# A new order for the opening of an attention and Fourier mixing kernel, with copies, queries, combinations and conversions of its first group at other places

## The chip, the cores and the metric

The kernel runs on one core of one Trainium2 chip. The metric is device time in microseconds (us), the median of the runs shown; lower is better. One further execution was taken under the hardware profiler, and all lines below that quote a trace come from it.

## The reference

The first stage is an attention whose softmaxes are taken over the query's features and over the key's positions, the second a Fourier mixing block with a two layer network. There are 8 batches of 576 positions and 8 heads of 64, so rows of 512:

```python
q_s = softmax(q, axis=-1)
k_s = softmax(k, axis=2)
kv = np.einsum('bhsd,bhse->bhde', k_s, v)
x = np.einsum('bhsd,bhde->bhse', q_s, kv)      # then laid out as (8, 576, 512)
...
mixed = np.real(np.fft.fft(np.fft.fft(x, axis=1), axis=2))
u = x + mixed
un = (u - mean(u)) / np.sqrt(var(u) + 1e-06)
out = u + np.maximum(un @ w_ch1, 0.0) @ w_ch2  # 512 to 2048 to 512
```

(Both softmaxes subtract the maximum and add 1e-9 to the sum; `softmax` stands for those three lines.) All is float32; the host hands the two weight matrices over as 64 bit words, and the kernel converts them to float32.

## The kernel before

**Tiling.** Each batch has 576 positions. Four tiles of 128 of them, called (c, u) with c and u in 0 and 1, are a batch's own; the other 64 of each batch are put together with those of the next batch into a "shared" tile of 128. The own tokens of a batch make a group of 512 columns for the network. There are nine groups: group 0 is batch 0, the eight others follow, the last two of them being the shared tokens and batch 7.

**Stages.** The opening (`opening`, L576, with `first_keys`, L516) does the attention of batch 0, its Fourier mixing (`folded`, `block`, `mix_own`) and its normalisation (`norm`, L1070). In the opening the four own query tiles are called A (0, 0), B (1, 1), C (0, 1) and D (1, 0), and the shared one t. Keys and values of batch 0 and 1 are k00 to k03 and k10 to k13: for each the maximum (max), the exponential (exp), four transposes (turn), their copy out of PSUM (four), and the product with v (kv, L560). "k0 last" and "k0 fifth" handle the last positions of all four, "k0 inverse" and "k0 scale" (L564) finish the key times value matrix. A query has max, less (subtract), exp, turn, copy, ones (L880, its sums), kv (L888), inverse and out (L903). Then tokens, columns, by and again (L949 to L969) fold rows and columns, b0 to b4 (L1001, L1004) are the first Fourier product, m0 and m1 (L1029, with sums in L1046) the second, and s, root, scales, normal (L1100 on VectorE, L1103 on ScalarE), turn (L1109) and laid (L1117) are the normalisation and its transposes for the network.

The first group of the network (`plain`, L1154) uses plain products: 16 blocks of L1163, each with a relu on ScalarE (L1168), then 64 products L1175 into four PSUM banks, in the order of the list DOWN. During this group the weights are converted for the first time (`weights`, L329; conversion i is c_i: L376 on ScalarE, L370 and L373 on VectorE, L377 on ScalarE, L378 on GpSimd; 0 to 15 are the first matrix and 16 to 31 the second), and the sums of weight blocks that the later groups need are formed and stored to DRAM (`combine`, L396: four L428 on VectorE and the stores L431 to L437; layer 0 writes w1s, layer 1 writes w2s, eight p of each). The attention and the mixing of batch 1 run beside it. The later groups use a fast matrix product with seven products for eight (`strassen`, L1192; L1237 in the first layer, L1448, L1333 and L1363 in the second), whose weights come from DRAM through `load` (L449, issued at L455).

**What sets the order.** No scheduler decides. Every step has a time in a list; the kernel sorts the steps by it and issues them (end of the main function), and each engine takes its own instructions strictly in that order. In the opening the times stand in the string OPENING. WARM adds, at the given times, so many matmuls that are not used (L242). After the opening the times are offsets from `first` (start of the first group) and t = first + second (start of its second half). DMAs are issued in the same way from the queue of SyncE (SP), a few in the opening from that of ScalarE.

**Buffers that matter.** The transposes have two PSUM banks (tag tr), the products acc three. Query tiles have three buffers (tag q) and their transposes two (qT). The combinations for p = 2 and 6 of layer 1 write to s1 and u2, which the fast product uses too; the others write to parts of the first matrix that are no longer needed, or to the buffer unT that is not yet used. The slots into which `load` writes are parts of that same first matrix.

## Time and profile before

| | before |
|---|---|
| median of 3 runs | 1087.71 us (1086.84 to 1087.93) |
| the profiled execution | 1088.17 us |
| its span, first to last instruction | 1086.4 us |
| mean granted TensorE clock | 0.997 |
| matmul passes | 6390 |
| DMA traffic | 236.29 MB, mean 218 GB/s |

The same by stage (busy us, from the windows of the trace):

| stage | us | TensorE | VectorE | ScalarE | GpSimd | GB/s |
|---|---|---|---|---|---|---|
| opening | 0 to 54.6 | 46.72 | 36.37 | 32.13 | 14.66 | 246 |
| first group, L1163 | 54.6 to 112.2 | 57.41 | 44.67 | 35.96 | 26.86 | 247 |
| first group, L1175 | 112.2 to 188.1 | 72.16 | 64.34 | 33.37 | 16.34 | 249 |
| second group | 188.1 to 307.3 | 119.20 | 69.20 | 43.91 | 51.45 | 224 |
| the rest | 307.3 to 1086.4 | 768.36 | 453.30 | 260.04 | 351.71 | 209 |

How to read it: a busy time is a sum over the instructions of an engine; a matmul in float32 is recorded as two passes, and neighbouring passes overlap a little, so TensorE's busy time says that it was working, not that it worked at its peak. In the lines of the trace that follow, "x8" counts passes. The name after an arrow in brackets is what ended the idle time before an instruction. The clock is a share of full speed.

### The profile page before, as it was taken

The page shows a single profiled execution, that of the slowest core. Times are in us where ns is not written, and L with a number is a line of the kernel's source. Part 1 is how long each engine was busy: PE and PEld are TensorE (multiplying, and loading weights), DVE is VectorE, ACT ScalarE, POOL GpSimd, SP SyncE. Part 2 cuts the span into 40 slices and gives each one's busy share as a digit, 9 for nine tenths or more (in the row PEclk, how much of TensorE's full clock was granted, in tenths as well). Part 3 has the DMA queues.
Part 4 walks back from the last instruction along what each step waited for, and adds up shares of the span by engine and source line. Part 5 has one row for each costly group of instructions (what it writes and reads, how often), then busy time and mean ns, then how long its engine had stood idle before and what let it go on. Part 6 is the DMA issues. An engine that isn't in the chain of part 4 may idle for free.

```text
span 1086.4 us, 16999 instructions
## 1 busy us (share of the span) xinstructions
PE 1063.9 (98%) x6390; PEld 922.5 (85%) x6390; DVE 667.9 (61%) x1285; ACT 405.4 (37%) x962; POOL 461.0 (42%) x377
## 2 busy tenths in 40 slices
PE   8899999999999999999999999999999999999997
PEld 7744454988888899889998998889988998899896
DVE  5877896565465775667654765677447742562251
ACT  5674732552235215531444234521552132131200
POOL 3153220146323644354624642374336353553343
PEclk9999999999999999999999999999999999999999
DMA  9477577466996567645765566557644674666473
GB/s 337 158 233 271 217 261 241 148 219 202 294 315 234 186 227 261 207 159 210 262 220 189 185 235 219 186 208 253 219 165 155 214 248 159 219 236 214 165 244 125
DMA packets 114785, 236.29 MB, mean 218 GB/s; under 512 B 24320, under 2 KB 76160, under 8 KB 104080
## 3 DMA queue, kind: packets, MB, share of 16 engines
q1 hardware_dynamic: 112896, 234.15, 63.2%
q10 hardware_dynamic: 1808, 1.06, 0.3%
q8 instruction: 51, 0.84, 0.3%
q14 instruction: 30, 0.25, 0.1%
HBM read 200.05 MB, written 39.32 MB: 220 GB/s over the span
## 4 chain that ended last, share of the span: by engine, by line
PE 83%; DVE 5%; ACT 2%; issue 1%; POOL 1%; DVEq 0%; ACTq 0%; POOLq 0%
PE bb L1237 15%; PE bb L1363 10%; PE bc L1237 10%; PE ba L1237 10%; PE bc L1363 6%; PE ba L1363 6%; PE bb L1333 4%; PE acc L717 2%; PE acc L888 2%; PE bb L1448 2%; PE bc L1175 2%; PE acc L1001 2%; PE acc L1004 2%; PE acc L1029 1%; PE bc L1448 1%; PE ba L1448 1%
## 5 line engine op out<-in xcount | busy, mean ns | idle before, releaser
L1237 PE MATMUL bb<-unT,big 128*128 128x256 f32 x768 | 183.9, 379 | 0.0
L384 POOL TENSOR_TENSOR big<-big 128x512 f32<-128x512 f32 x32 | 40.9, 1279 | 284.7 <-ACT big L1249 284.7
L1237 PEld LDWEIGHTS bb<-unT,big 128*128 128x128 f32 x768 | 142.8, 190 | 18.6 <-DVE u L1207 0.4
L1249 ACT ACTIVATE big<-big 128x512 f32<-128x512 f32 x96 | 60.4, 629 | 199.7 <-DVE big L1248 199.5
L1207 DVE TENSOR_TENSOR u<-bb,s 128x512 f32<-128x512 f32 x66 | 45.6, 691 | 131.1 <-PE bb L1237 113.8
L1237 PE MATMUL bc<-unT,big 128*128 128x256 f32 x512 | 123.9, 379 | 0.0
L1237 PE MATMUL ba<-unT,big 128*128 128x256 f32 x512 | 123.8, 379 | 0.0
L1363 PE MATMUL bb<-big 128*128 128x128 f32 x848 | 105.2, 275 | 2.3 <-DVE u L1370 2.3
L1237 PEld LDWEIGHTS ba<-unT,big 128*128 128x128 f32 x512 | 94.7, 190 | 12.4 <-issue 0.5
L1237 PEld LDWEIGHTS bc<-unT,big 128*128 128x128 f32 x512 | 94.4, 190 | 12.3 <-DVE big L1248 0.8
L1363 PEld LDWEIGHTS bb<-big 128*128 128x128 f32 x848 | 99.6, 192 | 2.9 <-DVE u L1370 2.9
L1309 DVE TENSOR_TENSOR big<-big 128x512 f32<-128x512 f32 x92 | 83.0, 945 | 5.9 <-POOL big L385 3.4
L1313 POOL TENSOR_TENSOR x<-x,big 128x512 f32<-128x512 f32 x52 | 68.0, 1318 | 28.0 <-ACT big L1340 14.8
L1363 PE MATMUL ba<-big 128*128 128x128 f32 x640 | 79.6, 275 | 0.0
L1363 PEld LDWEIGHTS ba<-big 128*128 128x128 f32 x640 | 76.3, 192 | 1.2
L770 ACT ACTIVATE q<-q,qm 128x64 f32<-128x64 f32 x240 | 65.2, 338 | 27.1 <-DVE qm L764 20.6
L1309 POOL TENSOR_TENSOR big<-big 128x512 f32<-128x512 f32 x26 | 41.2, 1596 | 74.1 <-DVE big L1309 53.8
L1370 DVE TENSOR_TENSOR u<-bb,s 128x256 f32<-128x256 f32 x40 | 16.9, 423 | 70.5 <-PE bb L1363 61.8
L1333 PE MATMUL bb<-big 128*128 128x256 f32 x256 | 58.7, 380 | 0.0
L1248 DVE TENSOR_TENSOR big<-bc,u 128x512 f32<-128x512 f32 x64 | 44.0, 687 | 23.7 <-PE bc L1237 22.6
L1333 PEld LDWEIGHTS bb<-big 128*128 128x128 f32 x256 | 48.2, 190 | 8.0 <-DVE big L1248 1.1
L1363 PE MATMUL bc<-big 128*128 128x128 f32 x416 | 51.5, 275 | 0.0
(260 smaller groups left out, 2030.9 us busy)
## 6 DMA issues: line engine op xcount, KB each, us to landing
big<-w2d SPq DMA_DIRECT2D x67, 1024.0 KB, 4.8
big<-w1s SPq DMA_DIRECT2D x64, 896.0 KB, 4.9
big<-w2s SPq DMA_DIRECT2D x16, 1024.0 KB, 6.3
big<-in_w_dram SPq DMA_DIRECT2D x21, 512.0 KB, 6.2
w2d<-big SPq DMA_DIRECT2D x42, 256.0 KB, 5.6
q<-in_q_dram SPq DMA_DIRECT2D x27, 256.0 KB, 6.5
k<-in_kT_dram SPq DMA_DIRECT2D x24, 288.0 KB, 5.7
v<-in_v_dram SPq DMA_DIRECT2D x24, 256.0 KB, 3.6
```

Source lines behind the costliest of these rows:

```text
L384: e1.tensor_tensor(out=to(4), in0=at(2), in1=at(3), op=ALU.add)
L717: nc.tensor.matmul(pk, lhsT=ks[:, c, :], rhs=v[:, c, :], start=(c == 0), stop=(c == NC - 1))
L770: nc.scalar.activation(q[:, h, :], q[:, h, :], ACT.Exp, bias=m[:, h:h + 1])
L1207: plus = lambda t: V.tensor_tensor(out=temp(t), in0=box["bb"][:], in1=box["s1"][:], op=ALU.add)
L1237: nc.tensor.matmul(bank()[:, i, :], lhsT=w[:, WA_AT[m], k * P:(k + 1) * P], rhs=self.unT[g][:, B_AT[m], k, :], start=first and i == 0 and ...
L1248: steps = [(0, lambda: V.tensor_tensor(out=hp(i), in0=bank()[:], in1=u()[:], op=ALU.add)), (0.8, lambda: nc.scalar.activation(hp(i), hp(i) ...
L1249: (0.8, lambda: nc.scalar.activation(hp(i), hp(i), ACT.Relu))]
L1309: e.tensor_tensor(out=to(o), in0=to(x), in1=to(y), op=op)
L1313: G.tensor_tensor(out=x, in0=x, in1=tile(m), op=ALU.add)
L1333: nc.tensor.matmul(box[name][:, i, :], lhsT=h[p][:, A_AT[m], i * P:(i + 1) * P], rhs=self.stream[n][:, p, :], start=p == 0 and (m != 1 or ...
L1363: nc.tensor.matmul(box[place[n]][:, i, :], lhsT=own(m)(A_AT[n])[:, f, :], rhs=w[:, r // 2, r % 2 * P:r % 2 * P + P], start=first and f == ...
L1448: nc.tensor.matmul(bank()[:, i, :], lhsT=h[p][:, A_AT[m], i * P:(i + 1) * P], rhs=w[:, p, :], start=first and i == 0 and p == 0, stop=p == ...
```

## The change

The string OPENING and the list WARM are new. In the opening the shared query tile t is handled after the four own ones, and by a subtraction on VectorE and one exponential over 512 columns in place of eight of 64 with a bias each. The load of its first rows (`shared_firsts`) moves from ScalarE's queue to SP's, ahead of the two tables. Two of the four laid copies (those with c equal to u) are done by VectorE and not ScalarE. `first` is 46.9 in place of 48.2, so that all later times move with it. In the first group: conversion 1 is 2.2 later (relative to `first`), the conversions from 23 on are at other times, the combinations p = 6 and 7 of layer 0 come 24.5 later, those of layer 1 in another order and six of them close together near its end, three `load`s at other times, and the queries of batch 1 some 1 to 2.5 earlier; the fourth of these takes a q buffer in place of a piece of unT and is loaded 5.5 earlier.

```diff
--- before.py
+++ after.py
@@ -82,31 +82,30 @@
 PAIRS = [(j + NP // 2, j) for j in range(NP // 2)]
 
 DOWN = [(i, f) for n in range(4) for i in (2, 3, 0) for f in range(4 * n, 4 * n + 4)] + [(1, f) for f in range(NF)]
-WARM = (3, 3), (8.1, 1), (10.85, 1), (26.6, 2), (29, 3), (41.3, 3), (42.8, 2)
+WARM = (3, 3), (24.7, 6), (41.9, 2), (43.45, 1), (44.5, 1), (45.5,2)
 OPENING = """
-4.50 k00 max, 5.30 k00 exp, 5.50 k01 max, 6.25 k00 turn, 6.30 k01 exp, 6.50 k02 max, 7.15 k00 four,
-7.25 k01 turn, 7.60 k03 max, 7.65 k02 exp, 8.41 k01 four, 8.60 k02 turn, 8.91 k03 exp, 9.50 A max,
-9.67 k02 four, 9.86 k0 last, 10.10 B max, 10.25 A less, 10.36 k03 turn, 10.70 k0 fifth, 11.01 k03 four,
-11.29 B less, 11.30 k0 inverse, 11.50 t max, 11.51 A exp, 11.60 k00 kv, 12.25 A turn, 12.25 t exp0,
-12.70 k01 kv, 12.73 t exp1, 13.21 t exp2, 13.40 D max, 13.69 t exp3, 14.00 C max, 14.15 D less, 14.17 B exp,
-14.60 t inverse, 14.67 A copy, 14.82 B turn, 15.19 C less, 15.30 D exp, 15.32 A ones, 15.80 B copy,
-16.12 k02 kv, 16.23 t normal, 16.34 C exp, 16.77 D turn, 16.85 A inverse, 17.22 t turn, 17.72 k03 kv,
-17.87 t copy, 18.37 B ones, 18.52 k0 scale0, 18.97 k0 scale1, 19.17 C turn, 19.32 B inverse, 19.62 A kv,
-19.72 t fold, 20.32 k10 max, 20.42 t join, 20.59 B kv, 20.72 D copy, 20.99 A out, 21.22 k10 exp, 21.56 D ones,
-21.98 C copy, 22.03 B out, 22.36 D kv, 22.65 D inverse, 23.05 k11 max, 23.33 C ones, 23.72 D out,
-23.85 k11 exp, 24.13 C kv, 24.34 C inverse, 24.74 tokens1, 25.10 k11 turn, 25.36 C out, 25.55 k10 turn,
-25.70 k11 four, 25.98 columns1, 26.00 t kv, 26.20 k10 four, 26.34 tokens0, 26.96 tokens2, 27.05 t parts,
-27.58 columns0, 28.06 by1, 28.15 c0 hi, 28.42 by0, 28.78 t folds, 28.80 c0 lo, 29.53 again0, 29.83 again1,
-30.33 tokens3, 30.43 b1 times, 30.95 columns2, 31.31 columns3, 31.41 b4 times, 31.63 b1 copies, 31.79 by3,
-32.15 by2, 32.39 b0 times, 32.61 b4 copies, 32.63 again2, 32.93 again3, 33.43 k13 max, 33.53 b3 times,
-33.59 b0 copies, 34.10 c0 shift, 34.23 k13 exp, 34.51 b2 times, 34.80 c0 sign, 34.99 b3 copies, 35.40 k12 max,
-35.49 k13 turn, 35.52 c0 add, 35.71 b2 copies, 36.26 k12 exp, 36.41 m0 times, 37.02 k13 four, 37.31 k12 turn,
-37.52 m0 copy, 37.76 m1 times, 37.91 k12 four, 38.02 m0 sums, 38.66 k1 last, 38.86 m1 copy, 38.92 m0 add0,
-39.26 k1 fifth, 39.60 m0 add1, 39.60 m1 sums, 39.76 roots, 39.91 k10 kv, 40.40 s00, 40.66 k11 kv,
-40.90 m1 add1, 41.15 s01, 41.41 k12 kv, 42.05 root0, 42.16 k13 kv, 42.20 m1 add0, 42.88 scales0, 43.08 s10,
-43.23 normal01, 43.83 s11, 43.98 turn01, 44.58 normal00, 44.73 root1, 44.93 laid01, 45.08 scales1,
-45.23 turn00, 45.43 normal10, 45.43 normal11, 45.98 laid00, 46.08 turn10, 46.68 turn11, 46.83 laid10,
-47.43 laid11, 49.00 k1 inverse, 49.30 k1 scale0, 49.60 k1 scale1"""
+4.30 k00 max, 5.10 k00 exp, 5.50 k01 max, 6.05 k00 turn, 6.30 k01 exp, 6.65 k02 max, 7.06 k00 four,
+7.25 k01 turn, 7.56 k02 exp, 7.75 k03 max, 8.32 k01 four, 8.51 k02 turn, 8.82 k03 exp, 8.90 A max, 9.50 B max,
+9.58 k02 four, 9.65 A less, 9.77 k0 last, 10.10 k0 inverse, 10.27 k03 turn, 10.42 k0 fifth, 10.69 B less,
+10.80 A exp, 11.20 k00 kv, 11.30 k03 four, 11.84 B exp, 11.85 A turn, 12.20 C max, 12.30 k01 kv, 12.45 A copy,
+12.80 D max, 12.95 B turn, 12.95 C less, 13.40 A ones, 13.55 B copy, 13.99 D less, 14.10 C exp, 14.20 k02 kv,
+14.35 A inverse, 14.85 C turn, 15.00 t max, 15.14 D exp, 15.30 k03 kv, 15.75 t less, 15.95 D turn,
+16.35 k0 scale0, 16.40 B ones, 16.47 t exp, 16.80 k0 scale1, 17.14 t inverse, 17.25 B kv, 17.99 B inverse,
+18.22 A kv, 18.35 C copy, 18.39 t normal, 19.01 B out, 19.19 t turn, 19.32 D copy, 19.63 k10 max, 19.69 C ones,
+19.84 t copy, 20.30 A out, 20.43 k10 exp, 20.49 C kv, 20.92 C inverse, 21.39 t fold, 21.46 D ones,
+22.09 t join, 22.26 D kv, 22.51 D inverse, 22.91 C out, 23.31 t kv, 23.53 D out, 24.15 tokens0, 24.21 k10 turn,
+24.36 t parts, 24.77 tokens1, 25.39 columns0, 25.46 k10 four, 25.75 columns1, 26.23 by1, 26.59 by0,
+26.80 c0 hi, 26.95 t folds, 27.45 c0 lo, 27.70 again0, 28.00 again1, 28.50 tokens3, 28.60 b0 times,
+29.12 tokens2, 29.58 b1 times, 29.74 columns3, 29.80 b0 copies, 30.10 columns2, 30.56 b4 times, 30.58 by2,
+30.78 b1 copies, 30.94 by3, 31.42 again2, 31.72 again3, 31.76 b4 copies, 32.22 k12 max, 32.32 b2 times,
+32.89 c0 shift, 33.02 k12 exp, 33.30 b3 times, 33.59 c0 sign, 33.78 b2 copies, 34.19 k13 max, 34.28 k12 turn,
+34.31 c0 add, 34.50 b3 copies, 34.86 k11 max, 35.05 k13 exp, 35.20 m0 times, 35.81 k12 four, 36.10 k13 turn,
+36.31 m0 copy, 36.55 m1 times, 36.66 k11 exp, 36.81 m0 sums, 37.42 k13 four, 37.61 k1 last, 37.71 m0 add0,
+37.92 m1 copy, 38.07 k11 turn, 38.27 k1 fifth, 38.39 m0 add1, 38.42 m1 sums, 38.77 k11 four, 38.92 k10 kv,
+39.22 s00, 39.27 roots, 39.67 k11 kv, 39.69 m1 add1, 39.97 s01, 40.42 k12 kv, 40.87 root0, 40.99 m1 add0,
+41.17 k13 kv, 41.67 scales0, 41.87 s11, 42.02 normal01, 42.62 s10, 42.77 turn01, 43.37 normal00, 43.52 root1,
+43.87 scales1, 43.89 normal11, 43.95 laid01, 44.02 turn00, 44.22 normal10, 44.77 laid00, 44.87 turn10,
+45.47 turn11, 45.62 laid10, 46.22 laid11, 51.00 k1 inverse, 51.30 k1 scale0, 51.60 k1 scale1"""
 ATT_EPS = 1e-9
 LN_EPS = 1e-6
 
@@ -272,7 +271,7 @@
                 nc.scalar.dma_start(tail[i * Q:(i + 1) * Q], flat[a:a + Q])
 
         def shared_firsts():
-            nc.scalar.dma_start(tail[0:P:Q], self.q[b:b + 2].rearrange("b s n -> (b s) n")[::S // 2])
+            load(tail[0:P:Q], self.q[b:b + 2].rearrange("b s n -> (b s) n")[::S // 2])
 
         def table():
             t = self.small.tile([P, 1], F32, tag="root", name="root", bufs=1)
@@ -298,9 +297,9 @@
             load(t[:, 4, :], self.v[1, S - P:, cols])
 
         order = [lambda: nc.gpsimd.memset(v[0:64, 4, :], 0.0), shared, table, *(lambda r=r: keys(r) for r in range(NR)), lambda: queries(0),
-                 lambda: values(0), lambda: queries(1), lambda: values(2), self.tables,
+                 lambda: values(0), lambda: queries(1), lambda: values(2), shared_firsts, self.tables,
                  *(lambda r=r: second(r) for r in range(NR)), *(lambda i=i: fetch(i) for i in range(11))]
-        return [(8.3, shared_firsts)] + [(i / 100, step) for i, step in enumerate(order)]
+        return [(i / 100, step) for i, step in enumerate(order)]
 
     def shared(self, a, b):
 
@@ -591,7 +590,7 @@
             for name, (_, step) in zip(names, script):
                 steps[name] = step
 
-        named("t max,t exp0,t exp1,t exp2,t exp3", self.q_exp(shared)[:-1])
+        named("t max,t less,t exp", self.q_exp_spread(shared, V))
         named("t inverse,t normal", self.q_inverse(shared, V, V))
         named("t turn,t copy", self.t_turn(shared))
         named("t fold,t join", self.t_fold(shared))
@@ -733,10 +732,7 @@
             if b == 0:
                 self.live[it] = [self.at_start[2][c ^ u][:, u, :]]
                 return
-            if b == 1 and (c, u) == (1, 1):
-                q = self.spare(D)
-            else:
-                q = self.work.tile([P, D], F32, tag="q", name="q", bufs=3)[:]
+            q = self.work.tile([P, D], F32, tag="q", name="q", bufs=3)[:]
             self.nc.sync.dma_start(q, self.q[b, tokens(c, u), :])
             self.live[it] = [q]
 
@@ -799,7 +795,7 @@
 
         return [(0, inverse), (0, times)]
 
-    def q_exp_spread(self, it):
+    def q_exp_spread(self, it, e=None):
 
         nc, live = self.nc, self.live
         heads = lambda: live[it][0].rearrange("p (h d) -> p h d", h=H)
@@ -811,7 +807,7 @@
 
         def less():
             m = live[it].pop()[:].unsqueeze(2).to_broadcast([P, H, DH])
-            nc.gpsimd.tensor_tensor(out=heads(), in0=heads(), in1=m, op=ALU.add)
+            (e or nc.gpsimd).tensor_tensor(out=heads(), in0=heads(), in1=m, op=ALU.add)
 
         def exp():
             q = live[it][0]
@@ -1114,7 +1110,8 @@
                 self.unT[g] = self.work.tile([P, 7, 2, HD], F32, tag="unT", name="unT", bufs=1)
             c, u = i % 2, i // 2
             cols = slice(c * P, (c + 1) * P)
-            nc.scalar.copy(self.unT[g][:, u:u + 3:2, :, cols], box.pop(i)[:].rearrange("p (a k) t -> p a k t", a=2))
+            copy = V.tensor_copy if g == 0 and c == u else nc.scalar.copy
+            copy(self.unT[g][:, u:u + 3:2, :, cols], box.pop(i)[:].rearrange("p (a k) t -> p a k t", a=2))
 
         def combine():
             if g > 0:
@@ -1549,7 +1546,7 @@
         return lazy(lambda: blk.combine(layer, p), 0, 0.4, 0.8, 1.2, 2.2)
 
     groups = [*range(B - 1), B, B - 1]
-    first, second, both = 48.2, 56, 77
+    first, second, both = 46.9, 56, 77
     steps = blk.opening(fetch, converted)
     up, down = blk.plain(0, lambda: blk.unT[0])
     for f in range(NF):
@@ -1557,21 +1554,21 @@
     t = first + second
     for i, some in enumerate(down):
         steps += at(t + 1.2 * i, some)
-    words = [first - 1.9, *(first + 0.9 + 1.7 * i for i in range(NF - 2))]
-    words += [first + dt for dt in (27, 31, 35, 39, 44, 49)] + [t + dt for dt in (-2, 3, 8, 12, 15, 17.2, 29, 32, 35, 38)]
+    words = [first + 0.3, *(first + 0.9 + 1.7 * i for i in range(NF - 2))]
+    words += [first + dt for dt in (27, 31, 35, 39, 44, 49)] + [t + dt for dt in (-2, 2, 5.5, 9, 12, 26, 30, 33, 36, 39)]
     for i, dt in enumerate(words, 1):
         steps += at(dt, converted(i))
-    for p, dt in enumerate((15, 20, 25, 36, 41, 46.5, 59, 62.5)):
+    for p, dt in enumerate((15, 20, 25, 36, 41, 46.5, 83.5, 87)):
         steps += at(first + dt, combined(0, p))
     steps += [(t + 0.5 + 0.1 * i, lambda i=i: fetch(i)) for i in LATE_WORDS]
     steps.append((t + 6, lambda: setattr(blk, "spare_words", blk.raws[LATE_WORDS[0]].bitcast(F32))))
-    steps += [(t + 14 + 4 * i, lambda i=i: blk.load(i)) for i in range(3)] + [(t + 71, lambda: blk.load(3))]
-    for p, dt in zip((3, 0, 1, 7, 2, 4, 5, 6), (30.5, 33.5, 37, 45, 50, 56, 61, 65)):
+    steps += [(t + dt, lambda i=i: blk.load(i)) for i, dt in ((1, 14), (0, 36), (2, 40))] + [(t + 71, lambda: blk.load(3))]
+    for p, dt in zip((3, 7, 0, 1, 2, 4, 5, 6), (34, 42.5, 57.3, 59.3, 61.3, 63.5, 65.5, 68)):
         steps += at(t + dt, combined(1, p))
     own = [("q", 1, c, u) for c in range(2) for u in range(2)]
     for i, it in enumerate(own):
-        at_q = t - 14 + 6 * i
-        steps += at(t - 34 + i if i < 3 else t + 0.6, blk.q_load(it)) + at(at_q, blk.q_exp(it))
+        at_q = t - 15 + 5.5 * i
+        steps += at(t - 34 + i if i < 3 else t - 4.9, blk.q_load(it)) + at(at_q, blk.q_exp(it))
         steps += at(at_q + 9.5, blk.q_turn(it)) + at(at_q + 14, blk.q_times_kv(it))
     steps += at(t + 11, blk.t_times_kv(1)) + at(t + 19.5, blk.folded(1))
     for k, dt in zip((2, 3, 0, 1, 4), (25, 26.5, 29.5, 31, 32.5)):
```

## The prediction

> **What bounds the kernel now.** I read the page first (parts 1 and 2), then who TensorE waited for, then the opening and the first group engine by engine in order of time, then the granted clock by microseconds.

> ```profile
> span 1086.4 us, 16999 instructions
> ...
> PE 1063.9 (98%) x6390; PEld 922.5 (85%) x6390; DVE 667.9 (61%) x1285; ACT 405.4 (37%) x962; POOL 461.0 (42%) x377
> ...
> PE   8899999999999999999999999999999999999997
> ```

> TensorE is busy nearly throughout, and no matmul of the reference is added or removed. So the change can win only where TensorE stands idle or runs slowly: in the opening, before the first L1163 matmul at 54.59, and in the waits of the first group. From 188 us on, TensorE waits only 3.3 us in all (2.3 of it L1363 on DVE), and its order there is untouched. The waits from 54 to 190 us are these (total, times, longest):

> ```profile
> PE acc L1001 <- DVE eo L969: 1.7, 1, 1.7
> PE ba L1163 <- ACT unT L1117: 1.5, 1, 1.5
> PE acc L888 <- DVE big L373: 1.1, 1, 1.1
> PE tr L826 <- issue: 0.6, 1, 0.6
> ...
> PE acc L888 <- ACT qT L836: 0.2, 1, 0.2
> ```

> All but the L1163 line lie between 112 and 141 us, where VectorE is 34.69 us busy of 38; the chain that ended last runs on DVE (L428, L370, L764, L787) from 95 to 140.5. There DVE is the bound.

> The first block of eight L1163 passes (a start, a length) takes 5.37 us, and every later one 3.60; the windows show why (PEclk is the number after POOL's):

> ```profile
> 54.59 5.37 PE L1163 MATMUL ba<-unT,big 128*128 128x512 f32 x8 [1.51 <-ACT unT L1117]
> 59.79 3.60 PE L1163 MATMUL bb<-unT,big 128*128 128x512 f32 x8
> ```
> ```profile
> 52.00:54.00 2.00, 0.66 (x4) 0.42 (x4) 1.03 (x2) 2.00 (x5) 0.00 (x0) 1.00 0.00 0
> ...
> 56.00:57.00 1.00, 1.00 (x2) 0.34 (x1) 0.97 (x3) 0.09 (x1) 0.00 (x0) 0.50 0.31 49
> 57.00:58.00 1.00, 1.00 (x2) 0.34 (x1) 0.97 (x3) 0.00 (x0) 0.81 (x1) 0.50 0.63 233
> ```

> TensorE was idle for most of 52 to 54.6, ACT busy all through, and the clock then fell to half for some 3.4 us: 1.75 us lost.

> [...]0.50 from about 55.3 to 58.7, and 128-column passes of 421 ns until about 14 us, 275 after. [...]here 1.28 at 44.09, before the first root. [...]here an L428 takes 0.41 alone and up to 1.57 beside L378. [...]the nearest row, L549 on DVE, took 0.70.

> **The opening, part by part.** The rows that I start from (ACT, then DVE):

> ```profile
> 8.86 1.13 ACTq L275 DMA_DIRECT2D big<-in_q_dram  x1
> 10.03 0.59 ACT L541 COPY ks<-tr 128x512 f32<-128x512 f32 x1 [1.54 <-PE tr L538]
> 14.82 2.02 ACT L770 ACTIVATE big<-big,qm 128x64 f32<-128x64 f32 x8 [0.64 <-DVE qm L764]
> ```
> ```profile
> 22.18 0.86 DVE L564 TENSOR_TENSOR kvr<-acc,kinv 64x256 f32<-64x256 f32 x2 [2.80 <-PE acc L560]
> 41.97 0.76 DVE L1046 TENSOR_TENSOR eo<-acc,sn 128x256 f32<-128x256 f32 x2 [1.68 <-ACT sn L1038]
> ```

> (1) L275 leaves ACT's queue, where the copy "k01 four" stood behind it until 10.03. It can now start when "k02 exp" ends, at 8.5. Then k03 exp ends at 9.9 (11.4 before), k0 last and k03 turn run cold (1.24 + 1.06) from 9.95, and k00 kv starts at 12.3 instead of 13.67: -1.4.
> (2) On TensorE, k00 kv still runs cold (2.1), then A turn 0.45, k01 kv 1.2, B turn 0.45, ones 0.9, k02 kv 1.2, C turn 0.45, k03 kv 1.15: end 20.2 against 21.98. The shared turn (0.44) and the 0.55 wait are no longer in it. The shared exponentials are one 0.63 instruction instead of 2.02, plus one DVE addition of 0.69 ahead of L564, in idle time. L564 ends at 21.1, not 23.04: -1.9.
> (3) DVE from L564 to "again1" took 11.3 (23.07 to 34.4). It gains the shared inverse 1.05 and normal 0.69, which stood before L564, and gives up k11 max 0.67 and one token sum 0.64: some 12.0. End 33.2: -1.2.
> (4) The token sum and k11 max come back before "again3": 37.1 against 37.64. On ACT, k13 exp 0.97 and k12 four 0.5 stand before m0 copy, so m0 sums (L1046) start at 41.8: -0.2 only. What is late next is ACT.
> (5) From L1046 to the second L1100 is as before, 8.25 (the table load on ACT ends at 46.1, just in time): 49.9, -0.3.
> (6) The tail took 4.37 before (50.22 to 54.59): ACT alone did four L1117 copies (0.58 each), the last L1103, and c1's L376 and L377 between them. Now copies 00 and 11 are on DVE at 0.70 each and c1 waits behind. From 49.9: copy 00 50.45 to 51.1, turn11 to 51.75, copy 11 to 52.45, beside it two warming matmuls (0.86) to 52.6. L1163 starts at 52.65: -1.9 in all.

> The warming matmuls stay 15 in number (0.43 each when warm). They fill the wait for DVE and now also the gaps between the four turns, so the idle window goes and with it the half clock: -1.75. Conversion c1 is due 3.43 after the start: L376 0.65, two L370 and one L373 2.0, L378 1.29 come to about that; +0.2.

> L275 on SP costs up to its 1.13 there, ahead of the tables, the second batch's keys and the words. I take nothing: the DMA share is above 1.0 until 36 us, so transfers and not issue are late. Without that cover: 1.1 on c0.

> **The first group.** Combinations (0,6) and (0,7) leave the stretch from 116 to 125.5: eight L428, 1.85 + 0.41 + 0.42 + 2.70 = 5.4 us of DVE. Conversion 27 (0.42 + 1.69) moves behind the folds. That is 7.5 us less before the L969 that TensorE waits for; the queries go in 1 to 2.5 earlier. Of the waits 1.70 + 1.13 + 0.55 + 0.17 = 3.55 I keep 0.5, for the fourth query, whose exponentials still queue on ACT with conversions: -3.0. The moved 7.5 us fit into DVE's idle time after 141: 1.14 + 3.59 + 4.61 = 9.3. Without it the subtractions L1123 are late for the second product of the next group.

> DMAs that move: the fourth query takes a q buffer, and its load waits for the first query's turn (108.2); behind it on SP are three late words, which before stood behind a load that went at 112.3. The loads of w1s 4 and 5 go some 18 to 22 us later, behind the stores of combinations 6 and 7. They land about 30 us before they are read: nothing.

> **Sum.** -1.9 - 1.75 + 0.2 - 3.0 = -6.45. The profiled execution took 1088.17 (span 1086.4 and 1.77 around it), 0.46 above the median 1087.71. From its own time: 1081.7; from the median: 1081.3, my forecast. Both ends of the unknowns: opening 0 to -3, half clock 0 to -1.75, waits 0 to -3.55, burst of stores 0 to +4. No end lies below the sum of the idle and slow time that exists.

> **Rivals.** (B) A half-clock window remains. The warming matmuls at 8 and 11 us are gone, and TensorE waits about 4 us near 29 to 33 with six warming matmuls in it[...]. For it: 41% busy sufficed for the fall at 55. Against: every gap is about half filled. 1.75 given back, and perhaps 0.7 of the opening: 1083.8.
> (C) The early start is eaten by DVE: its work from 54 to 140 must start as late as its words and relus allow, so L1001 waits for L969 again. Then the opening and the clock give nothing and only the moved combinations do, up to 3.0: 1084.7 to 1087.
> (D) Slower: six layer-two combinations now stand together late in the first group, 6 x 0.92 MB of stores, plus 1.3 MB of outputs, in some 18 us: 378 GB/s, where the best 5 us window carried 375. The last stores free s and u, which the next group's L1208 and L1207 write. L1208 ran 2.4 us after that group's start and the bank is wanted 5.7 after it; some 1.9 slack. Each us later is one us of TensorE. At 300 GB/s the burst costs 3; it ends above 1089.9 only if the last store lands more than about 12 us into the group. For it: nothing waits now, but the stores were spread over 45 us. Against: rates of 375 to 386 are held for long in the opening.

> **Numbers.** Forecast 0.58, at 1081.3, own range 1079.3 to 1083.3. B 0.20. C 0.14, half of it inside 0.2% (2.2 us, about what a measurement can tell). D 0.08. Faster 0.85 (0.58 + 0.20 + 0.07), same 0.07, slower 0.08. The range 1078.7 to 1085.8 leaves out 0.05 below, part of C and all of D.

> **What would show it.** Right: L541 for k01 near 8.5; L564 near 20.3; L1046 near 41.8; first L1163 near 52.7, with a block of 3.6; waits on DVE between 105 and 140 under 1 us; order-1 L1237 near 181.7 instead of 188.13. Wrong: PEclk under 1 after 15 us; L1001 waiting for L969; L1237 waiting for L1207 or L1123.

## The result and the profile after

The changed kernel takes 1080.04 us (median of 4 runs, 1079.32 to 1081.36) against 1087.34 for the kernel before beside it (1086.84 to 1087.93): ratio 0.9934, 95% interval 0.9917 to 0.9951, so 7.3 us faster. 1081.3 was forecast. The profiled execution took 1081.36 (1088.17 before). In the kernel after, the lines of the code have moved by one to four: L540 is what was L541, L563 L564, L1042 L1046, L1160 L1163, L1234 L1237. (opening_alone, below, lies between the two: its L968, L1000, L1163 and L1175 are L965, L997, L1160 and L1172 of the kernel after.)

Page, parts 1 and 2 of the kernel after:

```profile
span 1079.6 us, 16993 instructions
...
PE 1059.0 (98%) x6390; PEld 920.7 (85%) x6390; DVE 666.7 (62%) x1288; ACT 403.4 (37%) x953; POOL 459.9 (43%) x377
```

TensorE's busy time fell by 4.9 us with the same 6390 passes (2.4 in the opening, 2.5 in the first group), and fewer of them ran slowly: the clock rose to full at 5.89 us and not at 14.41, though it halved once after that, and the first block was no longer at half clock. The rest of the 6.8 us of the span is idle time.

Who TensorE waited for from 56 to 190 us in the kernel after (total, times, longest):

```profile
PE tr L822 <- DVE q L794: 1.1, 1, 1.1
PE acc L884 <- ACT qT L832: 0.9, 1, 0.9
PE tr L1105 <- ACT unT L1114: 0.4, 1, 0.4
```

The wait of 1.7 for L969 is gone, but 2.4 us are left where the prediction kept 0.5.

The opening of the kernel after: the copy k01 four on ACT, the scaling and the mixing on DVE, the first k00 kv and the first network products on PE (start, length):

```profile
8.86 0.56 ACT L540 COPY ks<-tr 128x512 f32<-128x512 f32 x1
```
```profile
19.02 0.86 DVE L563 TENSOR_TENSOR kvr<-acc,kinv 64x256 f32<-64x256 f32 x2 [0.98 <-PE acc L559]
...
40.01 0.76 DVE L1042 TENSOR_TENSOR eo<-acc,sn 128x256 f32<-128x256 f32 x2 [1.02 <-ACT sn L1034]
```
```profile
11.62 1.58 PE L559 MATMUL acc<-big,ks 128*128 128x128 f32 x8
...
51.33 3.67 PE L1160 MATMUL ba<-unT,big 128*128 128x512 f32 x8 [0.26 <-PE ba L241]
55.28 3.67 PE L1160 MATMUL bb<-unT,big 128*128 128x512 f32 x8 [0.28 <-DVE big L372]
```

The first network product starts 3.26 earlier, and its block takes 3.67 in place of 5.37: no half clock there. But the windows of the kernel after (PEclk is the number after POOL's) show that a half clock did occur, elsewhere:

```profile
10.00:11.00 1.00, 1.00 (x6) 0.58 (x5) 1.00 (x2) 0.66 (x3) 0.96 (x1) 0.50 1.05 384
11.00:12.00 1.00, 1.00 (x6) 1.00 (x5) 0.93 (x3) 0.76 (x2) 1.00 (x2) 0.50 1.09 390
```

The span in stages, before and after: to the first product 54.59 and 51.33 (-3.26); from there to the first product of the second group 133.54 and 129.85 (-3.69, of which 1.70 is the first block's clock); from there to the end 898.27 and 898.42. Nothing is given back later.

### The profile page after: what moved, and what is told of

Same layout as the page of the kernel before. It is cut to its first block, busy times and chain, and to the rows that moved or that the text cites. A ratio compares the mean times of both kernels' runs of the same rounds, so it can differ in the third digit from the quotient of the medians.

```text
span 1079.6 us, 16993 instructions
## 1 busy us (share of the span) xinstructions
PE 1059.0 (98%) x6390; PEld 920.7 (85%) x6390; DVE 666.7 (62%) x1288; ACT 403.4 (37%) x953; POOL 459.9 (43%) x377
## 3 DMA queue, kind: packets, MB, share of 16 engines
q10 hardware_dynamic: 1800, 1.05, 0.3%
## 4 chain that ended last, share of the span: by engine, by line
PE 84%; DVE 3%; ACT 2%; POOL 1%; issue 1%; DVEq 0%; ACTq 0%; POOLq 0%
PE bb L1234 15%; PE bb L1360 10%; PE bc L1234 10%; PE ba L1234 10%; PE bc L1360 6%; PE ba L1360 6%; PE bb L1330 5%; PE acc L716 2%; PE acc L884 2%; PE bc L1172 2%; PE bb L1445 2%; PE acc L997 2%; PE acc L1000 2%; PE acc L1025 1%; PE bc L1445 1%; PE ba L1445 1%
## 5 line engine op out<-in xcount | busy, mean ns | idle before, releaser
L1234 PE MATMUL bb<-unT,big 128*128 128x256 f32 x768 | 183.9, 379 | 0.0
L1234 PEld LDWEIGHTS bb<-unT,big 128*128 128x128 f32 x768 | 142.8, 190 | 18.6 <-DVE u L1204 0.4
L1234 PE MATMUL bc<-unT,big 128*128 128x256 f32 x512 | 124.0, 379 | 0.0
L1234 PE MATMUL ba<-unT,big 128*128 128x256 f32 x512 | 123.8, 379 | 0.0
L1234 PEld LDWEIGHTS ba<-unT,big 128*128 128x128 f32 x512 | 94.7, 190 | 12.4 <-issue 0.5
L1234 PEld LDWEIGHTS bc<-unT,big 128*128 128x128 f32 x512 | 94.4, 190 | 12.3 <-DVE big L1245 1.0
L1330 PE MATMUL bb<-big 128*128 128x256 f32 x256 | 58.7, 380 | 0.0
L1330 PEld LDWEIGHTS bb<-big 128*128 128x128 f32 x256 | 48.2, 190 | 8.0 <-DVE big L1245 1.1
```

Source lines behind the costliest of these rows:

```text
L1234: nc.tensor.matmul(bank()[:, i, :], lhsT=w[:, WA_AT[m], k * P:(k + 1) * P], rhs=self.unT[g][:, B_AT[m], k, :], start=first and i == 0 and ...
L1330: nc.tensor.matmul(box[name][:, i, :], lhsT=h[p][:, A_AT[m], i * P:(i + 1) * P], rhs=self.stream[n][:, p, :], start=p == 0 and (m != 1 or ...
```

## The experiments

My theory after the result: three savings, in the opening, in the clock and in the first group's order, that add. The rivals: that VectorE bounds the first group, so that an earlier opening is lost there (C of the prediction); and that the half clock isn't tied to the tail at all (the tail is the stretch from the end of the second L1096, L1100 before, to the first network product). "First product" and "distance" are the start of the first L1160 and from there to the first L1234 (L1163, L1237), from each profile. The last two columns are the clock records of the trace: when the first record, a rise to full clock, begins, and where a later record shows 0.50.

| kernel | median us | ratio to before (95%) | first product | distance | full clock from | half clock later |
|---|---|---|---|---|---|---|
| before | 1087.34 | | 54.59 | 133.54 | 14.41 | 55.37 to 58.78 |
| after | 1080.04 | 0.9934 (0.9917 to 0.9951) | 51.33 | 129.85 | 5.89 | 9.30 to 12.72 |
| after_again | 1079.70 | 0.9930 (0.9916 to 0.9945) | 49.91 | 129.35 | 6.76 | none |
| group_alone | 1085.26 | 0.9982 (0.9975 to 0.9989) | 54.64 | 129.71 | 5.57 | 12.39 to 15.80 |
| group_fill | 1084.57 | 0.9969 (0.9958 to 0.9981) | 55.02 | 129.41 | 5.24 | 12.06 to 15.48 |
| opening_alone | 1083.64 | 0.9965 (0.9952 to 0.9979) | 49.88 | 134.12 | 5.96 | 135.66 to 139.07 |
| before_fill | 1088.58 | 1.0010 (1.0003 to 1.0017) | 56.68 | 133.50 | 5.50 | 12.33 to 15.74, 142.03 to 145.45 |
| no_fill | 1082.50 | 0.9954 (0.9938 to 0.9970) | 50.49 | 130.46 | 11.75 | none |
| laid_act | 1080.78 | 0.9940 (0.9928 to 0.9953) | 50.07 | 130.59 | 10.86 | none |
| c1_early_act | 1082.26 | 0.9948 (0.9935 to 0.9960) | 51.72 | 129.67 | 5.92 | 9.33 to 12.74 |
| firsts_act | 1082.38 | 0.9959 (0.9946 to 0.9971) | 52.55 | 129.33 | 14.16 | none |
| combos_back | 1081.30 | 0.9944 (0.9930 to 0.9958) | 51.24 | 130.19 | 5.72 | 9.13 to 12.54 |
| mended | 1079.52 | 0.9923 (0.9910 to 0.9935) | 50.23 | 127.15 | 11.74 | none |
| mended_again | 1078.44 | 0.9915 (0.9901 to 0.9929) | 50.13 | 128.14 | 11.48 | none |

("None": up to the last product. Each ratio is to runs of the kernel before beside it, whose medians were 1087.34 for after, and 1087.16, 1087.17 and 1087.92. Ahead of the first record the traces have none, and the views put 1.00 there; the passes are slow in that stretch: four transposes took 1.06 us at 8.97 in before, and 0.66 at 8.46 in group_alone, whose opening is the same.)

**The two halves of the change.** group_alone is the kernel before with the part of the diff from `words` on and in `q_load`, conversion 1 left where it was; opening_alone is the changed kernel with that part undone:

```diff
-    words = [first + 0.3, *(first + 0.9 + 1.7 * i for i in range(NF - 2))]
+    words = [first - 1.9, *(first + 0.9 + 1.7 * i for i in range(NF - 2))]
```

(group_alone against the changed kernel: the one line of the first group in which the two differ.)

```diff
-    for p, dt in enumerate((15, 20, 25, 36, 41, 46.5, 83.5, 87)):
+    for p, dt in enumerate((15, 20, 25, 36, 41, 46.5, 59, 62.5)):
...
-        at_q = t - 15 + 5.5 * i
+        at_q = t - 14 + 6 * i
```

(opening_alone, two lines of it.)

> The kernel before, with only the first group's part of the change (conversions, combinations, loads and queries at the new times, the opening untouched). Theory, that the stages add: it takes away most of the waits between 112 and 141 us, the 1.7 of L1001 on DVE first, and nothing else: 1.5 to 2.5 us faster than before, 1085.3, with the L1163 start still at 54.6 and the half clock still there. As predicted (3.0 from the waits): 1084.3. Rival, that the waits only matter once the opening is early: within 0.5 us of before, 1087.

> The changed kernel with the first group's steps at the old times relative to its start (the new opening, filling matmuls, copies on two engines and the later conversion 1 stay). If the stages add: 3.3 of the opening and 1.7 of the clock, 1082.3. If VectorE bounds the first group (rival C of the prediction): its work from 54 to 140 us cannot start earlier by as much as the group does, the wait for L965 (L969 in the kernel before) grows from 1.7 by 2 to 4 us, and the time is 1084.5 to 1086.

Measured by the ratios: -2.0 and -3.8 us, 5.8 together, where the whole change gives 7.2 to 7.6. The intervals are wide enough for the two to add. In opening_alone the wait for L968 is still 1.71, not longer: rival C has fallen. But right behind it the clock halves, and four L1175 passes take 3.27 where four take 1.9 otherwise:

```profile
134.71 0.95 PE L1000 MATMUL acc<-ft,eo 128*128 128x144 f32 x4 [1.71 <-DVE eo L968]
...
136.29 3.27 PE L1175 MATMUL ba<-big 128*128 128x512 f32 x4
```
```profile
136.00:137.00 1.00, 1.00 (x3) 0.49 (x2) 0.97 (x4) 0.46 (x3) 0.00 (x0) 0.50 0.92 251
137.00:138.00 1.00, 1.00 (x3) 0.34 (x1) 0.97 (x3) 0.09 (x2) 0.00 (x0) 0.50 0.92 370
```

So there were two places where the clock could fall, the tail and the wait for L968. This trace pays at the second and the one of before paid at the first: its distance is 134.12, against 133.54.

**The clock at the tail.** group_alone kept the tail of before, with its idle 1.51 ahead of the first product, and yet shows no half clock there; one came at 12 to 16:

```profile
54.64 3.67 PE L1160 MATMUL ba<-unT,big 128*128 128x512 f32 x8 [1.51 <-ACT unT L1114]
```
```profile
13.00:14.00 1.00, 1.00 (x6) 1.00 (x6) 0.00 (x0) 0.46 (x1) 0.00 (x0) 0.50 0.95 369
...
56.00:57.00 1.00, 1.00 (x4) 0.52 (x3) 0.97 (x2) 0.16 (x1) 0.00 (x0) 1.00 0.28 33
```

In each of the fourteen profiles all changes of the clock lie a whole number of steps of 3.413 us apart (in before 12 steps from 14.41 to 55.37 and one more to 58.78; in opening_alone 38 from 5.96 to 135.66), while the first change comes at another time each time (5.24 to 14.41). So these steps lie elsewhere against the kernel's work in each of these executions. Here are such steps of before (the first three lines), of group_alone (two) and of opening_alone (one); the first number after the comma is TensorE's busy time in the step:

```profile
51.96:55.37 3.41, 1.44 (x6) 0.91 (x7) 2.25 (x6) 3.41 (x7) 0.88 (x1) 1.00 0.00 0
55.37:58.78 3.41, 3.41 (x5) 1.35 (x4) 2.91 (x5) 0.72 (x2) 1.69 (x2) 0.50 0.45 154
137.29:140.70 3.41, 1.71 (x5) 0.59 (x4) 3.27 (x9) 0.00 (x0) 0.41 (x1) 1.00 1.03 369
```
```profile
49.94:53.35 3.41, 2.42 (x18) 1.63 (x16) 0.69 (x2) 2.70 (x5) 0.00 (x0) 1.00 0.00 0
53.35:56.76 3.41, 2.12 (x5) 1.06 (x6) 3.16 (x8) 2.81 (x6) 1.30 (x1) 1.00 0.00 0
```
```profile
132.25:135.66 3.41, 1.70 (x7) 0.81 (x6) 3.27 (x11) 0.00 (x0) 0.00 (x0) 1.00 1.02 352
```

In before the tail's gap lay in one step, in which TensorE was busy 42% of the time, and the next step ran at half clock. In group_alone a border cut the same gap in two, the steps were 71% and 62% busy, and the clock stayed. The wait for L969 (L968) made a step about 50% busy: the clock fell after it in opening_alone and stayed in before. So the same gap cost in one execution and not in another: the first block took 5.37 in before and 3.67 in group_alone. Laid at all positions over the tail of before, a step is less than half busy (where half clock followed in these profiles; the last section has the shares) in 1.62 of every 3.41 us; from this I estimate that about half of the executions pay the 1.70 there, 0.8 us on average. The steps were found in the traces afterwards; no run could set where they lie.

Three more kernels bear on it. before_fill puts eleven more filling matmuls (two or three at each of four places) into the tail of before:

```diff
+WARM = (3, 3), (8.1, 1), (10.85, 1), (26.6, 2), (29, 3), (41.3, 3), (42.8, 2), (44.8, 2), (45.9, 3), (46.55, 3), (46.75, 3)
```

> The kernel before with eleven more filling matmuls between its four turns of the tail and after them, and nothing else. If the half clock of 55.3 to 58.7 comes from the idle window ahead of it: PEclk stays 1.00, the first block takes 3.6 and the time falls by 1.75, less what the last fillers overshoot (0 to 0.5): 1085.6 to 1086.1. Rival, that the fall has another cause: 1087.3 or more.

A miss: the matmuls took more than the gaps, the first product came 2.1 late, and the clock halved at 142, behind the wait for L969 that had cost no half clock in the profile of before. With the one at 12 this execution has two half clocks, so it isn't one dip that moves from place to place.

```profile
56.68 3.67 PE L1163 MATMUL ba<-unT,big 128*128 128x512 f32 x8
```
```profile
140.89 0.95 PE L1001 MATMUL acc<-ft,eo 128*128 128x144 f32 x4 [1.71 <-DVE eo L969]
...
142.29 3.46 PE L1175 MATMUL ba<-big 128*128 128x512 f32 x4
```

group_fill puts four into group_alone, sized to the gaps: `(46.3, 1), (47.5, 3)`.

> The kernel with the first group's part of the change alone (1085.26), and four filling matmuls more, one between the third and the fourth turn of its tail and three after the fourth, sized to the gaps of 0.53 and 1.51. Theory, that a half-clock window of about 3.4 us falls in one idle place per execution, at the tail in some and elsewhere in others: PEclk is 1.00 from 44 to 62, the time falls by part of the 1.75, the slow end of the 17 runs (86.2 to 87.0) most: 1084.3 to 1084.8. Rival 1, that the tail costs 1.75 in every execution: 1083.5. Rival 2, that it costs nothing unless the waits of the first group are there too: 1085.2.

0.7 less by the medians, 1.4 by the ratios, with overlapping intervals. That is the time of the first expectation and about the estimated 0.8, as far as this goes; the six runs lie between 1084.05 and 1085.09, while 6 of the 17 of group_alone were above 1086.2. no_fill takes the tail's fillers out of the changed kernel: `WARM = (3, 3), (24.7, 6), (41.9, 2)`.

> The changed kernel without the four filling matmuls due from 43.45 on (those at 24.7 and 41.9 stay). If the fillers take the half clock away: it comes back, PEclk near 0.5 for some 3 us after the start of the first group, the first block takes about 5.4 and the time rises by 1.0 to 1.7, to 1081.0 to 1081.7; the start itself may come 0.3 earlier, since the last fillers end after the last copy. Rival, that the shorter tail alone keeps the clock up: 0.3 faster or the same, 1079.8.

Its profile shows no half clock before the end, and from the second L1096 to the second block it takes 6.99, against 7.02 with fillers. Its median is nevertheless 2.5 higher. 3.3 us of the profiled execution lie outside the span, where the profile of after has 1.8; but over all runs 1.5 to 1.8 of the rise lie inside it (median spans of 1079.7, against 1078.3 for after and 1077.9 for after_again). What that is, these runs don't tell. Laid over its tail, a step of 3.41 is less than half busy in 0.74 of every 3.41 us (0.46 at the lowest), and with the fillers nowhere less than 0.89. So the fillers can matter to the clock, by my estimate 0.4 us on average (that share of the 1.70), but a profile in which the clock falls in this tail was not seen: that they keep it up is not shown.

**The copies on two engines.** laid_act: `copy = nc.scalar.copy`. c1_early_act has that too, and conversion 1 back at `first - 1.9`.

> The changed kernel with all four laid copies on ScalarE, the rest unchanged. Prediction's step (6): the copies on two engines give most of the 1.6 of the tail; all on ScalarE the first L1160 starts 0.6 to 1.2 later, 1080.6 to 1081.2. Rival: ScalarE has room in this tail and the fillers end later than the last copy anyway: within 0.3, 1080.0 to 1080.3.

> The changed kernel with all four laid copies on ScalarE and conversion 1 due 1.9 before the start of the first group again (0.3 after it in the changed one), so that its L375 and L376 stand between the copies as in the kernel before; the rest unchanged. Theory, that the tail was shortened by taking conversion 1 out of it and not by the two engines: second L1096 to first L1160 takes 3.7 to 4.1 instead of 3.0, the wait of the second block for L372 (0.8 with copies on ScalarE) goes to 0 to 0.3: net +0.2 to +0.6 against the run with the copies alone (1080.78), 1081.2. Rival, that the new order of PE's products in the tail did it: 3.0 stays, 1080.3 to 1080.8.

With all four on ScalarE the first product comes 3.00 after the second L1096 ends (47.07), against 3.07 in the changed kernel and 4.37 before: for the start, the second engine gives nothing. It gives 0.5 one block later, since conversion 1 begins on ScalarE after the copies:

```profile
50.07 3.67 PE L1160 MATMUL ba<-unT,big 128*128 128x512 f32 x8 [0.15 <-PE ba L241]
54.55 3.67 PE L1160 MATMUL bb<-unT,big 128*128 128x512 f32 x8 [0.80 <-DVE big L372]
```

Putting conversion 1 among them costs 0.47 (3.47), in ACT's queue (the median rose by 1.5 over laid_act, more than the 0.2 to 0.6 expected, with overlapping intervals):

```profile
49.42 0.65 ACT L375 ACTIVATE bb<-big 128x512 f32<-128x512 f32 x1
50.00 0.59 ACT L1114 COPY unT<-tr 128x512 f32<-128x512 f32 x1
50.48 0.68 ACT L376 ACTIVATE big<-big 128x512 int32<-128x512 uint32 x1
51.04 0.58 ACT L1114 COPY unT<-tr 128x512 f32<-128x512 f32 x1
```

That leaves 0.9 of the tail's 1.30 to the order: the first turn starts at 47.11, 1.15 ahead of the second L1096's end, and the last L1099 stands before all copies; before, products and fillers held the first turn until 49.96, 0.26 ahead. That remainder is argued from the traces; it was not tried alone.

**The load on ScalarE's queue.** firsts_act issues `shared_firsts` from ScalarE at 8.3 again.

> The changed kernel with the load of the shared query's first rows back on ScalarE's queue at 8.3, where it took 1.13 us; the rest unchanged. Prediction's step (1): the copy k01 four goes from 8.86 to about 10.0, the first kv from 11.6 to 12.7, and the delay goes through the whole opening: +1.1, 1081.1. Rival: it is absorbed before the first network product, by a wait for VectorE or a later load: within 0.3 of 1080.0.

```profile
8.73 1.13 ACTq L274 DMA_DIRECT2D big<-in_q_dram  x1
9.90 0.58 ACT L540 COPY ks<-tr 128x512 f32<-128x512 f32 x1 [1.51 <-PE tr L537]
```

k01 four goes from 8.86 to 9.90, L563 to 20.26 (17.57 to 19.02 in the nine other profiles of the new opening), the first product to 52.55, and the median rises by 2.3, with no overlap of the runs (1081.75 to 1084.11, against 1079.09 to 1081.36 for the nine of the changed kernel). It isn't absorbed: with 1.2 to 2.7 us in the profiles no other piece of the opening that was tried alone moved the first product as far. Part of the difference may be the clock, which was full only from 14.16 in this execution.

**The combinations.** combos_back: `(15, 20, 25, 36, 41, 46.5, 59, 62.5)`.

> The changed kernel with combinations 6 and 7 of layer 0 back at 59 and 62.5 after the start of the group (they are at 83.5 and 87 in it); the rest unchanged. As predicted: their eight L428, 5.4 us of VectorE in 116 to 125, make the L997 products wait for L965 again: +1.7 to +3.0, 1081.7 to 1083.0. Rival: VectorE has 3.6 us of gaps there in the changed kernel, which take them: within 0.5, 1080.0 to 1080.5.

The L997 products don't wait for L965. The wait that grew is that of the fourth query, 1.1 to 1.9:

```profile
PE tr L822 <- DVE q L794: 1.9, 1, 1.9
```

The distance rises by 0.34, the median by 1.3 with overlapping intervals: the rival was nearer.

**A mended version.** VectorE in the changed kernel, as the fourth query comes:

```profile
117.85 0.69 DVE L369 TENSOR_SCALAR big<-acc 128x512 int32<-128x512 int32 x1 [1.91 <-ACT acc L375]
...
119.18 0.68 DVE L783 TENSOR_REDUCE qrec<-q 128x8 f32<-128x512 f32 x1
```

VectorE stands idle for 1.91, in front of a conversion that waits for ScalarE, while the query's inverse (L783), whose exponentials ended at 117.2, is queued behind it. Order, not work, so:

```diff
-WARM = (3, 3), (24.7, 6), (41.9, 2), (43.45, 1), (44.5, 1), (45.5,2)
+WARM = (3, 3), (24.7, 6), (41.9, 2), (43.45, 1), (44.5, 1), (45.5, 1)
...
-    ... [t + dt for dt in (-2, 2, 5.5, 9, 12, 26, 30, 33, 36, 39)]
+    ... [t + dt for dt in (-2, 2, 6.6, 9.5, 12, 26, 30, 33, 36, 39)]
...
-        ... at(at_q, blk.q_exp(it))
+        ... at(at_q - (0, 0, 0.9, 0.9)[i], blk.q_exp(it))
```

> The changed kernel with three small moves: the exponentials of the third and fourth query of batch 1 0.9 earlier, conversion 24 1.1 later and conversion 25 0.5 later (so that the fourth query's inverse is not behind a conversion that waits for ScalarE), and one filling matmul fewer at the end of the tail. If the residual waits come from the order on ScalarE and VectorE and not from the amount of work: the waits of 0.9 (L884 on L832) and 1.1 (L822 on L794) go, and the first L1160 starts 0.3 earlier: 1.5 to 2.3 less, 1077.7 to 1078.5. Rival, that the amount of work sets them: the waits appear elsewhere, within 0.5 of 1080.0.

> The mended kernel once more beside the changed one on the same chip. From the distances of its profile (first L1160 to first L1234 127.15 against 129.85; 0.25 less in the tail) it should be 2.5 to 3 faster than the changed one, though the five runs before gave 0.5 to 1: 1077.2 to 1079.0. Rival, that something given back later hides it: within 0.7 of the changed kernel.

> The changed kernel once more, on the same chip as the other three, to have its spread and a second profile of it: 1079.3 to 1081.4. By the theory of the half-clock window its profile need not show the window at 9 to 13 us again, but everything from the scaling L563 to the first product of the second group should take the same time within 0.3: 20.99 to the first L1042, 129.85 from the first L1160 to the first L1234. Rival, that the opening differs from run to run throughout: other distances.

In mended the view of TensorE's waits lists none between 100 and 180 us (in mended_again two, of 0.5 and 0.3 us, at the turns L1105); the fourth query's turn follows without a gap:

```profile
117.70 1.02 PE L1172 MATMUL ba<-big 128*128 128x512 f32 x2
118.56 0.60 PE L822 MATMUL tr<-ident,q 128*128 128x128 f32 x4
```

Its distances are 127.15 and 128.14, against 129.85 and 129.35. Beside each other on one chip the medians are 1078.44 and 1079.70; over nine runs of each 1078.67 and 1079.70, about 1.0 less, though the ranges overlap (1077.16 to 1080.28; 1079.09 to 1081.36). It is the fastest kernel here. Less came of it than expected: 1079.52 in the first five runs, where 1077.7 to 1078.5 was expected, and beside the changed kernel 1.3 less instead of 2.5 to 3. The waits are gone in the traces; why the medians show less stays open.

after_again also shows what varies: from L563 to the first L1042 it takes 21.00 us, as the first profile's 20.99; but L563 stands at 17.60, not 19.02: in this execution the clock was full from 6.76 on, and no half clock fell into 9 to 13. The distance from the first L1160 to the first L1234, expected within 0.3, is 0.5 shorter.

## Why the prediction was right, point by point

The forecast held, and so did the kinds of gain: an earlier start, no half clock in the first block, fewer waits in the first group. Three terms of the sum were mis-sized, in opposite directions, and two causes misnamed.

- **(1) L275 leaves ACT's queue**: right in kind. k00 kv starts at 11.62, not 12.3 (-2.05 for -1.4): k0 last and k03 turn ahead of it took 1.95, not 2.30. firsts_act confirms the cause. The size varies by execution: k00 kv starts at 12.64 to 14.02 in the four profiles of the old opening, at 10.56 to 11.62 in the nine of the new one, and at 12.68 in firsts_act.
- **(2)**: L563 at 19.02, not 20.3. From k00 kv to there 7.40 (8.51 before); the prediction let k00 kv run cold (passes of 421 ns, as before 14 us in the kernel before) for 2.1, and it took 1.65. Both terms hang on the clock of this execution; in after_again, where it was full from 6.76, L563 stands at 17.60.
- **(3), (4)**: the stretch on DVE is as predicted (11.9 for 12.0), though the four terms that were named give only 11.7. What failed is "what is late next is ACT": k13 exp and k12 four cost the m0 sums nothing (4.32 from again3, 4.33 before). L1042 at 40.01, not 41.8.
- **(5)**: 8.25, as predicted. The table load on ACT took 1.28 in both profiles and ended at 45.37 before and at 44.03 after.
- **(6)**: the tail gave 1.30 (1.6 predicted), but not by the copies on two engines (0.69 each on VectorE, 0.70 predicted): laid_act has the same start without them.
- **The half clock**: 1.70 in the profile for 1.75 predicted. But the term took one execution for the kernel: where the steps lie differs, and in the median the tail is worth some 0.7 to 1.4 by group_fill, 0.8 by my estimate. The wait for L969 was a second such place, which the term didn't count and the whole change closes too. And the idle window of the prediction wasn't needed: after a step that was busy for 1.70 of 3.41 us (opening_alone) the clock fell too. Rival B, that such a window remains, happened in the first profile, in the opening, where it cost up to 1.4 (19.02 against 17.60).
- **Conversion 1**: 0.28 for 0.2.
- **The first group**: -1.99 with conversion 1's 0.28 in it, for -2.8 predicted. "There DVE is the bound" was too strong: the 34.69 us of 38 beside it are those of 112 to 150 us; from 112 to 141 DVE is busy 27.06 of 29. The L969 wait went (1.70), but the queries wait for 2.0, not 0.5: the term assumed that less work on VectorE would serve them, and what held them was the order behind waiting conversions, as mended shows. The named cause, the 5.4 us of combinations, wasn't needed for the L969 wait. Whether conversion 27 or the earlier queries removed it was not tried.
- **Rival D**, the stores: didn't come: the view of TensorE's waits lists none from 180 to 320 us.

In the sum of the two profiles: -3.26 (predicted -1.9), -1.70 (-1.75), -1.99 (-2.8), +0.15 after: -6.80 against -6.45. It came that close by luck: too little in the opening and too much in the first group offset each other, and both are single executions: the first product comes at 49.88 to 51.33 in the four profiles with the new opening as it is, and at 54.59 to 55.02 in three with the old one.

## What to carry to other kernels

When a clock dip follows an idle gap in one profile, look for every other gap of that size, and don't take the dip's price for the gap's: here the steps of the clock lay elsewhere in each execution, and the idle 1.51 of the tail cost 1.70 in before and nothing in group_alone. Where an engine that takes its work in order stands idle in front of a waiting instruction (here VectorE for 1.91), look at the order first: with the work behind it moved ahead, TensorE's wait of 1.1 for the fourth query was gone from the trace. And look at what stands in the queue behind a DMA that a compute engine issues: here 1.13 us of ScalarE delayed the whole opening and cost 2.3 us of the median.
